# Softmax sums as identity matmuls in the logit bank, and a first inverse step of 64-partition matmuls in two banks

## The chip, the core and the metric

The kernel runs on one core of one Trainium2 chip. The engines that matter are TensorE (matmuls, PE in the profile; its weight loads are PEld), VectorE (DVE), ScalarE (ACT), GpSimd (POOL) and SyncE (SP), whose queue issues nearly all DMA transfers. Matmul results land in PSUM, a memory of eight banks of 2 KB for each of 128 partitions; VectorE and ScalarE read them from there. The metric is device time in microseconds of one execution, and the median of several runs is quoted.

## What is computed

Four layers on x of 2048 positions by 512 channels: attention, convolution, attention, convolution, each added to its layer-normed input. Cut to what the change touches:

```python
# attention: 32 heads of 16, each position looks at itself and at 7 earlier ones, 2 apart
qkv = (x @ wqkv).reshape(B, S, 3, H, Dh)
idx = pos[:, None] - off[None, :]              # off = 0, 2, ..., 14
logits = einsum("bhsd,bhswd->bhsw", q, kg) * scale
attn = softmax(where(mask, logits, -1e9), axis=-1)   # over the 8 keys w
o = einsum("bhsw,bhswd->bhsd", attn, vg)
return o @ wo
# convolution: y = irfft(rfft(u, 2L) * rfft(K, 2L))[:L] + u * Dskip, per channel, L = 2048,
# K = Re sum_n C_n exp(dt A_n l) dt B_n
```

Both attention layers share their weights, and both convolutions share the kernel K.

## The kernel before

**Start (0 to 112 us).** `k_gen` builds the taps K with powers of exp(dt A) and, in between, the first layer's norm, keys and queries. The order of all engines but GpSimd is written out by hand, one letter for each step (ORDERK here; ORDER0, ORDERF, ORDER1 for the convolutions).

**Attention (`LayerA.core`).** A block q is 512 positions, held as four rows of 128 partitions (a position's row is its index modulo 16, so rows 2 apart hold neighbours in the window). The program order is the order on each engine. For blocks 0 to 2, in slots (q, ft) with ft = 0 to 3: `mult` (L295, VectorE) multiplies queries with 8 shifted keys into `prod`; `lsum` (L302, TensorE) sums each head's 16 channels into the logits `L`, a PSUM tile of two banks laid out (row, key w, head), two tiles in turn; projections of values and queries (L351, L185) are put between. One block behind, `mx` takes the maximum over the keys (L365, VectorE), `sub_exp` subtracts it by an identity matmul (L372) and exponentiates into `ex` (L375, ScalarE), `recip` sums `ex` over the keys and makes rs = exp(-ln(sum)) (L381, L383, L385 on VectorE, L386 and L388 on ScalarE), and `norm_p` multiplies `ex` by rs into `attn` (L394, VectorE). For block q-1 `recip` stands after `lsum(q, 2)` and `norm_p` after `lsum(q, 3)`.

Then a loop over n = 0 to 15 goes through the rows, even ones mostly apart from odd ones at the start (0, 2, 1, 3, 4, ...): `pv_mult` (L404, VectorE, 2.28 us) multiplies weights and shifted values into `pav`, two buffers; `pv_sum` (L414, TensorE, 64 matmuls of 64 partitions, over two banks in turn) sums over the keys and transposes; ScalarE copies that to `oT` (L417); `out_proj` (L424, L426) projects it and adds x; ScalarE writes x back with its sums (L432, L108). Blocks 2 and 3 finish inside this loop: `recip` at n = 2 and n = 10, `norm_p` at n = 4 and n = 11. A position p x 16 + a lies in partition p of row a, so windows that reach back over row 0 need values of the partition before: two pairs of DMA copies `v_ext<-v_ext` (L356, L357), for even rows and for odd rows, each issued on SP when the last value projection of its kind is copied. The third pass of the loop (row 1) is the first that needs the odd ones. In layer 0 the loop also carries the loading and reordering of the taps (L1281, L1355) and sines for a table (L702).

**Convolution (`FftB`).** A transform of length 4096 in two steps each way. Channels come in two groups g of 256. K and U: `f1` (L758) copied by L747; k and u: `f2` (L765), copied by L747 or L820; m: `u_mult` (L807, VectorE) makes the products t1, t2 (the transform of the signal times that of the taps and its rotated partner, from the buffers `kf_ring`); y: `i1` (L833, L834), the first inverse step, 8 steps t to a group, copied to `z` by L747; z: `i2` (L857 to L859), the second inverse step, added to x (L862 on VectorE, or L864 on ScalarE with x added by an identity matmul). The letter after a token names the engine that copies: A ScalarE, D VectorE. "z01" is `i2` of group 0, quarter 1. All of these share accumulators of two banks each, four in turn, so step n waits until what step n-4 left has been copied out.

In a step of `i1` each of eight sets of four channels multiplies all 128 partitions of t1 and t2 with a table of 128 columns. Of these columns, each partition fills only the 32 that belong to its own channel of four (the mask `dmask_m`, L619, L666).

At the end of layer 0's convolution (ORDERF) the next attention layer's norm, transposes and key projections follow at once; layer 1's (ORDER1) ends with the stores of the output.

Of the kernel before, what the change touches and what calls it, by code (L numbers as in the profile page):

```python
# [10 lines left out]
ACT = mybir.ActivationFunctionType  # L11
ALU = mybir.AluOpType
# [3 lines left out]
BF16 = mybir.dt.bfloat16  # L16
# [4 lines left out]
P = 128  # L21
S = 2048
D = 512
H = 32
DH = 16
W = 8
# [15 lines left out]
DQT = 8  # L42
# [120 lines left out]
class LayerA:  # L163
# [143 lines left out]
    def core(self, x_sb, u, lnp, ev=None, nprod=0):  # L307

        tc, nc, lnst, l = self.tc, self.nc, self.lnst, self.layer
        ident, nident = self.c["ident"], self.c["nident"]  # L310
# [5 lines left out]
        st, linit, mult, lsum = self.st, self.linit, self.mult, self.lsum  # L316
# [5 lines left out]
        with ExitStack() as c2:  # L322
# [7 lines left out]
            wk = c2.enter_context(tc.tile_pool(name=f"a{l}_wk", bufs=2, reuse_waits="tile"))  # L330
# [45 lines left out]
                st[q]["ex"] = ex  # L376

            def recip(q):
                ex = st[q]["ex"]
                s4 = wk.tile([P, 4, 4, H], BF16, name="s4", bufs=1)  # L380
                nc.vector.tensor_tensor(s4[:], ex[:, :, 0:4, :], ex[:, :, 4:8, :], ALU.add)  # L381
                s2 = wk.tile([P, 4, 2, H], BF16, name="s2", bufs=1)
                nc.vector.tensor_tensor(s2[:], s4[:, :, 0:2, :], s4[:, :, 2:4, :], ALU.add)  # L383
                ssum = wk.tile([P, 4, 1, H], F32, name="ssum")
                nc.vector.tensor_tensor(ssum[:], s2[:, :, 0:1, :], s2[:, :, 1:2, :], ALU.add)  # L385
                nc.scalar.activation(ssum[:], ssum[:], ACT.Ln)  # L386
                rs = wk.tile([P, 4, 1, H], BF16, name="rs", bufs=1)
                nc.scalar.activation(rs[:], ssum[:], ACT.Exp, scale=-1.0)  # L388
                st[q]["rs"] = rs
# [114 lines left out]
            rows = [0, 2, 1, *range(3, NA)]  # L504
            for n in range(16):
# [3 lines left out]
                if n in (2, 10):  # L509
                    recip(2 + n // 8)  # L510
# [72 lines left out]
def iota_f32(nc, pool, name, n, step=1, base=0, channel_multiplier=0, parts=P):  # L583
    ti = pool.tile([parts, n], I32, name=name + "_i")
    nc.gpsimd.iota(ti[:], pattern=[[step, n]], base=base, channel_multiplier=channel_multiplier)
    tf = pool.tile([parts, n], F32, name=name)
    nc.scalar.copy(tf[:], ti[:])
    return tf


def build_b_consts(nc, cpool, tmp, w2_dram):
    C = {}
    EQ = P // 4
    base = tmp.tile([P, EQ, 16], I32, name="w2_base", tag="w2_base")
    pi_i = tmp.tile([P, 1], I32, name="p_i")
    nc.gpsimd.iota(pi_i[:], pattern=[[0, 1]], base=0, channel_multiplier=1)
    e21 = iota_f32(nc, tmp, "e21", P, step=256, base=128)
    aidx = iota_f32(nc, tmp, "aidx", 16, step=4096)
    d4i = iota_f32(nc, tmp, "d4i", 4)
    nc.gpsimd.iota(base[:], pattern=[[16, EQ], [4096, 16]], base=8, channel_multiplier=0)  # L600
    zt = tmp.tile([P, 1024], BF16, name="w2_zero")
    nc.gpsimd.memset(zt[:], 0.0)
    t_i = tmp.tile([P, 8], I32, name="pk_t")
# [2 lines left out]
    nc.vector.tensor_scalar(t_i[:, 2:3], pi_i[:], 3, None, ALU.bitwise_and)  # L606
    nc.vector.tensor_scalar(t_i[:, 3:4], pi_i[:], 31, 1, ALU.bitwise_and, ALU.logical_shift_right)
    nc.vector.tensor_scalar(t_i[:, 4:5], pi_i[:], 1, None, ALU.bitwise_and)
    nc.vector.tensor_scalar(t_i[:, 5:6], pi_i[:], 5, None, ALU.logical_shift_right)
    nc.vector.tensor_scalar(t_i[:, 6:7], pi_i[:], 63, 1, ALU.bitwise_and, ALU.logical_shift_left)  # L610
    nc.vector.tensor_copy(t_i[:, 7:8], pi_i[:])
    pk = tmp.tile([P, 8], F32, name="pk"); nc.vector.tensor_copy(pk[:], t_i[:])
# [2 lines left out]
    aux = cpool.tile([P, 8], F32, name="aux")  # L615
    nc.vector.tensor_tensor(aux[:, 0:1], pk[:, 6:7], rik, ALU.add)
    nc.vector.tensor_scalar(aux[:, 1:2], pf, 2.0, 1.0, ALU.mult, ALU.add)
    C["p21"] = aux[:, 1:2]
    dmask_m = aux[:, 4:8]  # L619
    nc.vector.tensor_scalar(dmask_m, d4i[:], d4m, 2.0 / 4096.0, ALU.is_equal, ALU.mult)  # L620

    f1t = [tmp.tile([P, P], I32, name=f"f1_t{j}") for j in range(2)]
# [8 lines left out]
    def rest():  # L631
# [14 lines left out]
        ws, w2q = {}, {}  # L646
# [15 lines left out]
            sine(ws[name][:], low16(wt[name][:].rearrange("p r a -> p (r a)")))  # L662

        def w_mask(name):
            C[name] = cpool.tile([P, 32, 4], BF16, name=name)
            nc.gpsimd.tensor_tensor(C[name][:], ws[name][:].unsqueeze(2).to_broadcast([P, 32, 4]),  # L666
                                    dmask_m.unsqueeze(1).to_broadcast([P, 32, 4]), ALU.mult)

        def w2_store():
            for s in range(4):  # L670
# [5 lines left out]
        steps += [lambda nm=nm, t=t: f1_sine(nm, t) for nm, t in zip(("F1c", "F1s"), f1t)]  # L676
        steps += [w2_sine] + [lambda name=name: w_sine(name) for name, offs in wps]
        C["masks"] = lambda: [w_mask(name) for name, offs in wps]
        return steps, w2_store

# [27 lines left out]
class FftB:  # L708
# [113 lines left out]
    def i1(self, g, t, eng):  # L822
        nc, C = self.nc, self.C
        if t == 0:
            self.S[g]["z"] = self.z0 if g == 0 else self.gtile("z", [P, 2 * NA, DQG * 4])
        z = self.S[g]["z"]
        t1, t2 = self.S[g]["t"]
        wp_r = C["Wp"][:].rearrange("p m d -> p (m d)")
        wpj_r = C["WpJ"][:].rearrange("p m d -> p (m d)")
        p3 = self.ptile([P, DQT, P])  # L830
        for j in range(DQT):
            dql = t * DQT + j
            nc.tensor.matmul(p3[:, j, :], lhsT=t1[:, dql, :], rhs=wp_r, start=True, stop=False)  # L833
            nc.tensor.matmul(p3[:, j, :], lhsT=t2[:, dql, :], rhs=wpj_r, start=False, stop=True)  # L834
        self.evac(z[:, :, t * DQT * 4:(t + 1) * DQT * 4].rearrange("p m (j d) -> p m j d", d=4),
                  p3[:].rearrange("p j (m d) -> p m j d", d=4), eng)

    def i2(self, g, t, eng):

# [447 lines left out]
def kernel(  # L1287
# [38 lines left out]
    with tc.manual_schedule(engines=MAN):  # L1326
        C = k_gen(tc, nc, consts["ident"], ins, kd, la, x_v, lnst, lambda sp: build_b_consts(nc, cpool, sp, w2_dram))
# [153 lines left out]
```

## Time and profile before

| what | us |
|---|---|
| median of 3 runs (424.58 to 425.59) | 424.74 |
| the profiled execution, whole | 425.23 |
| its span, first to last instruction | 423.40 |
| VectorE busy | 396.5 |
| TensorE matmuls busy | 337.9 |
| ScalarE busy | 321.7 |
| L381, L383, L385 (VectorE, 8 each), median of one | 0.418, 0.293, 0.292 |
| L833, L834 (TensorE, 256 each), mean of one | 0.219 |
| L747 into z on ScalarE (12), on VectorE (4), mean of one | 1.03, 1.22 |

Matmuls are pipelined: one takes 0.219 us from start to end, but the next starts well before. What a row of them costs is read from start to start. A line of the timeline gives start, length, engine, line, operation, output and input, and in brackets how long the engine had been idle and what ended that. The stretches that matter: 118 to 141 the logits of layer 0, 141 to 197 its loop, 199 to 262 the first convolution, 262 to 316 front and logits of layer 1, 314 to 372 its loop, 373 to 419 the second convolution.

### The profile page before, as it was taken

How to read it: one execution, taken by the hardware profiler on the slowest of the kernel's cores; microseconds unless marked ns; L12 is line 12 of the kernel's file. 1: busy time of each engine (PE TensorE's matmuls, PEld its weight loads, DVE VectorE, ACT ScalarE, POOL GpSimd, SP SyncE). 2: the span in 40 equal slices, each digit the busy share in tenths (PEclk: the TensorE clock that was granted, in tenths of full speed). 3: DMA queues.
4: the chain of work that ended last, by engine and by line, in shares of the span. 5: the costliest groups of instructions: out<-in, count | busy, mean ns of one | idle time of the engine just before them, and what ended most of it. 6: DMA issues, size and time to landing. Idle time of an engine off the chain costs nothing.

```text
span 423.4 us, 14780 instructions
## 1 busy us (share of the span) xinstructions
PE 337.9 (80%) x6530; PEld 239.4 (57%) x6530; DVE 396.5 (94%) x539; ACT 321.7 (76%) x552; POOL 43.9 (10%) x46
## 2 busy tenths in 40 slices
PE   3000179999999879779998999999997878996995
PEld 2000036657765555546887898555654655576894
DVE  8999999999999999997999958889899999989975
ACT  5999998986455478987999988764555658679962
POOL 3000300000499000000500000000000020000000
PEclk9999999999999898999999999999999999999999
DMA  8940742122014855393244692730033036515406
GB/s 205 394 121 12 76 85 70 32 59 70 18 43 116 219 149 169 103 378 104 78 152 178 224 324 58 241 108 2 2 98 79 3 145 269 185 59 165 137 17 185
DMA packets 62458, 54.30 MB, mean 128 GB/s; under 512 B 33877, under 2 KB 50874, under 8 KB 61114
## 3 DMA queue, kind: packets, MB, share of 16 engines
q1 hardware_dynamic: 62250, 53.22, 41.4%
q8 instruction: 51, 0.84, 0.9%
q10 hardware_dynamic: 144, 0.13, 0.3%
q14 instruction: 13, 0.11, 0.1%
HBM read 30.28 MB, written 13.24 MB: 103 GB/s over the span
## 4 chain that ended last, share of the span: by engine, by line
PE 33%; DVE 28%; ACT 8%; DMA 6%; SPq 5%; issue 5%; DVEq 0%; ACTq 0%
DVE pav L404 11%; DVE t L807 5%; PE pk L1176 4%; DVE a1s L747 4%; PE pp L1114 4%; PE pq L351 3%; PE pp L242 3%; SPq L1198 3%; PE L L302 2%; PE pq L185 2%; PE pb L834 2%; PE pb L833 2%; PE pq L426 2%; PE po L414 2%; DMA kf_ring<-kf_dram 2%
## 5 line engine op out<-in xcount | busy, mean ns | idle before, releaser
L404 DVE TENSOR_TENSOR pav<-attn,v_ext 128x4096 bf16<-128x4096 bf16 x32 | 72.9, 2282 | 0.2 <-PE pq L426 0.2
L295 DVE TENSOR_TENSOR prod<-qT,kT_ext 128x4096 bf16<-128x4096 bf16 x29 | 66.4, 2307 | 0.2
L414 PE MATMUL po<-ident,pav 64*128 64x64 bf16 x2048 | 36.6, 192 | 16.8 <-DVE pav L404 10.9
L414 PEld LDWEIGHTS <-pav 64*128 64x128 bf16 x2048 | 33.2, 96 | 28.8 <-DVE pav L404 22.0
L1104 PE MATMUL pt<-ident,x_blk 128*128 128x128 bf16 x64 | 6.8, 259 | 43.1 <-ACT x_blk L158 43.1
L1016 DVE TENSOR_TENSOR A_t<-A_t,pow_t 128x1024 bf16<-128x1024 bf16 (+4 forms) x46 | 38.3, 874 | 0.2
L426 PE MATMUL pq<-wop,oT 128*128 128x512 bf16 x128 | 34.6, 395 | 0.0
L820 ACT CAST ub<-pb 128x1024 bf16<-128x1024 f32 x32 | 32.5, 1056 | 1.4 <-DVE t L807 0.6
L353 ACT CAST v_ext<-pq 128x512 bf16<-128x512 f32 x32 | 18.7, 586 | 19.3 <-PE pq L351 18.1
L302 PEld LDWEIGHTS <-prod 128*128 128x128 bf16 x928 | 26.7, 96 | 9.5 <-DVE prod L295 4.8
L1114 PE MATMUL pp<-xnT,kT_ext 128*128 128x512 bf16 x96 | 29.2, 436 | 3.4 <-ACT xnT L1107 1.7
L1104 PEld LDWEIGHTS <-x_blk 128*128 128x128 bf16 x64 | 5.5, 118 | 46.0 <-ACT x_blk L158 44.0
L765 PE MATMUL pb<-a1s,w_sb 128*128 128x64 bf16 x768 | 27.3, 193 | 5.2 <-ACT a1s L747 2.9
L833 PE MATMUL pb<-Wp,t 128*128 128x128 bf16 x256 | 30.4, 219 | 1.2 <-ACT xnT L747 0.5
L834 PE MATMUL pb<-WpJ,t 128*128 128x128 bf16 x256 | 30.0, 219 | 1.1 <-DVE t L807 1.1
L351 PE MATMUL pq<-wv,xnT 128*128 128x512 bf16 x128 | 30.7, 379 | 0.0
L747 DVE CAST a1s<-pb 128x1024 bf16<-128x1024 f32 x23 | 27.0, 1213 | 3.8 <-PE pb L758 3.8
L765 PEld LDWEIGHTS <-w_sb 128*128 128x128 bf16 x768 | 24.7, 98 | 7.5 <-issue 5.8
L302 PE MATMUL L<-ind,prod 128*128 128x8 bf16 x928 | 27.5, 166 | 1.3 <-DVE prod L295 1.1
L747 ACT CAST a1s<-pb 128x1024 bf16<-128x1024 f32 x25 | 24.9, 1036 | 2.5 <-PE pb L758 2.2
L834 PEld LDWEIGHTS <-t 128*128 128x128 bf16 x256 | 24.9, 98 | 3.2 <-DVE t L807 1.5
L417 ACT CAST oT<-po 128x512 bf16<-128x512 f32 x32 | 18.4, 576 | 9.7 <-PE po L414 9.4
(227 smaller groups left out, 864.4 us busy)
## 6 DMA issues: line engine op xcount, KB each, us to landing
w_sb<-w_dram SPq DMA_DIRECT2D x8, 1024.0 KB, 7.3
w_dram<-w_zero SPq DMA_DIRECT2D x1, 4096.0 KB, 14.4
kf_ring<-kf_dram SPq DMA_DIRECT2D x13, 256.0 KB, 3.7
kf_ring<-kf_dram SPq DMA_DIRECT2D x26, 128.0 KB, 3.6
v_ext<-v_ext SPq DMA_DIRECT2D x4, 784.0 KB, 6.3
x_blk<-in_A_x_dram SPq DMA_DIRECT2D x4, 512.0 KB, 4.3
kT_ext<-in_A_wqkv_dram SPq DMA_DIRECT2D x4, 512.0 KB, 9.3
x_sb<-in_A_x_dram SPq DMA_DIRECT2D x4, 512.0 KB, 7.0
```

The costliest lines, as they stand in the source:

```text
L295: nc.vector.tensor_tensor(pr, self.qT[q][:, ft].unsqueeze(1).to_broadcast([P, W, 4, P]), kap, ALU.mult)
L302: self.nc.tensor.matmul(L[:, al, w, ft * 8:(ft + 1) * 8], lhsT=pr[:, w, al, :], rhs=self.c["ind8"][:], start=(ft == 0 and w == 0 and al % ...
L351: nc.tensor.matmul(pp[:], lhsT=xnT[:, dt, a * P:(a + 1) * P], rhs=wv[:, dt, :], start=(dt == 0), stop=(dt == NDT - 1))
L404: nc.vector.tensor_tensor(pv[:], attn[:, n % 4].unsqueeze(2).to_broadcast([P, W, DH, H]), vap, ALU.mult)
L414: nc.tensor.matmul(po[:, h, 0, ft, :], lhsT=pvf[rows, w, ft * P:(ft + 1) * P], rhs=ident[rows, rows], start=(w == 0 and ft == 0), stop=(w ...
L426: nc.tensor.matmul(pw[:], lhsT=oT[:, ftp, :], rhs=self.wo[:, ftp, :], start=False, stop=(ftp == NDT - 1))
L747: (self.nc.scalar.copy if eng == "act" else self.nc.vector.tensor_copy)(dst, src)
L765: nc.tensor.matmul(p2[:, j, :], lhsT=self.w2[:, ec * EC + j, :], rhs=a1s[:, ec * EC + j, :], start=True, stop=True)
L833: nc.tensor.matmul(p3[:, j, :], lhsT=t1[:, dql, :], rhs=wp_r, start=True, stop=False)
L834: nc.tensor.matmul(p3[:, j, :], lhsT=t2[:, dql, :], rhs=wpj_r, start=False, stop=True)
L1016: return lambda: nc.vector.tensor_tensor(*args)
L1114: nc.tensor.matmul(pps[kind, b, ft][:], lhsT=la.wqk[:, dt, c:c + P], rhs=la.xnT[:, dt, b * 512:(b + 1) * 512], start=(dt == 0), stop=(dt = ...
```

## The change

The three VectorE adds in `recip` go. In their place eight matmuls with the identity add the eight keys of `ex` in PSUM, into the first 128 columns of the block's own logit tile, whose content `ex` has replaced. The Ln on ScalarE reads the sum from there.

In `i1` each matmul of 128 partitions and 128 columns becomes two, of partitions 0 to 63 and 64 to 127 and of 64 columns, with the outputs in two different banks. The table has 64 columns: of a half's partitions each fills the 32 of its own channel of two. The mask and the copies to `z` follow the new layout.

With the smaller tiles the buffers behind them take other addresses, and with them the waits of some DMA issues: in SP's queue of layer 1 the load of `g2_sb` now stands ahead of the `kf_ring` loads, and two of those loads stand between the two pairs of `v_ext` copies. The order on the compute engines is as before but for the instructions named.

```diff
--- before.py
+++ after.py
@@ -376,14 +376,12 @@
                 st[q]["ex"] = ex
 
             def recip(q):
-                ex = st[q]["ex"]
-                s4 = wk.tile([P, 4, 4, H], BF16, name="s4", bufs=1)
-                nc.vector.tensor_tensor(s4[:], ex[:, :, 0:4, :], ex[:, :, 4:8, :], ALU.add)
-                s2 = wk.tile([P, 4, 2, H], BF16, name="s2", bufs=1)
-                nc.vector.tensor_tensor(s2[:], s4[:, :, 0:2, :], s4[:, :, 2:4, :], ALU.add)
+                ex, L = st[q]["ex"], st[q]["L"]
+                tot = L[:, 0, 0:4, :]
+                for w in range(W):
+                    nc.tensor.matmul(tot, lhsT=ident[:], rhs=ex[:, :, w, :], start=(w == 0), stop=(w == W - 1), skip_group_check=True)
                 ssum = wk.tile([P, 4, 1, H], F32, name="ssum")
-                nc.vector.tensor_tensor(ssum[:], s2[:, :, 0:1, :], s2[:, :, 1:2, :], ALU.add)
-                nc.scalar.activation(ssum[:], ssum[:], ACT.Ln)
+                nc.scalar.activation(ssum[:, :, 0, :], tot, ACT.Ln)
                 rs = wk.tile([P, 4, 1, H], BF16, name="rs", bufs=1)
                 nc.scalar.activation(rs[:], ssum[:], ACT.Exp, scale=-1.0)
                 st[q]["rs"] = rs
@@ -596,7 +594,7 @@
     nc.gpsimd.iota(pi_i[:], pattern=[[0, 1]], base=0, channel_multiplier=1)
     e21 = iota_f32(nc, tmp, "e21", P, step=256, base=128)
     aidx = iota_f32(nc, tmp, "aidx", 16, step=4096)
-    d4i = iota_f32(nc, tmp, "d4i", 4)
+    d4i = iota_f32(nc, tmp, "d4i", 2)
     nc.gpsimd.iota(base[:], pattern=[[16, EQ], [4096, 16]], base=8, channel_multiplier=0)
     zt = tmp.tile([P, 1024], BF16, name="w2_zero")
     nc.gpsimd.memset(zt[:], 0.0)
@@ -606,7 +604,7 @@
     nc.vector.tensor_scalar(t_i[:, 2:3], pi_i[:], 3, None, ALU.bitwise_and)
     nc.vector.tensor_scalar(t_i[:, 3:4], pi_i[:], 31, 1, ALU.bitwise_and, ALU.logical_shift_right)
     nc.vector.tensor_scalar(t_i[:, 4:5], pi_i[:], 1, None, ALU.bitwise_and)
-    nc.vector.tensor_scalar(t_i[:, 5:6], pi_i[:], 5, None, ALU.logical_shift_right)
+    nc.vector.tensor_scalar(t_i[:, 5:6], pi_i[:], 5, 1, ALU.logical_shift_right, ALU.bitwise_and)
     nc.vector.tensor_scalar(t_i[:, 6:7], pi_i[:], 63, 1, ALU.bitwise_and, ALU.logical_shift_left)
     nc.vector.tensor_copy(t_i[:, 7:8], pi_i[:])
     pk = tmp.tile([P, 8], F32, name="pk"); nc.vector.tensor_copy(pk[:], t_i[:])
@@ -616,7 +614,7 @@
     nc.vector.tensor_tensor(aux[:, 0:1], pk[:, 6:7], rik, ALU.add)
     nc.vector.tensor_scalar(aux[:, 1:2], pf, 2.0, 1.0, ALU.mult, ALU.add)
     C["p21"] = aux[:, 1:2]
-    dmask_m = aux[:, 4:8]
+    dmask_m = aux[:, 4:6]
     nc.vector.tensor_scalar(dmask_m, d4i[:], d4m, 2.0 / 4096.0, ALU.is_equal, ALU.mult)
 
     f1t = [tmp.tile([P, P], I32, name=f"f1_t{j}") for j in range(2)]
@@ -662,9 +660,9 @@
             sine(ws[name][:], low16(wt[name][:].rearrange("p r a -> p (r a)")))
 
         def w_mask(name):
-            C[name] = cpool.tile([P, 32, 4], BF16, name=name)
-            nc.gpsimd.tensor_tensor(C[name][:], ws[name][:].unsqueeze(2).to_broadcast([P, 32, 4]),
-                                    dmask_m.unsqueeze(1).to_broadcast([P, 32, 4]), ALU.mult)
+            C[name] = cpool.tile([P, 32, 2], BF16, name=name)
+            nc.gpsimd.tensor_tensor(C[name][:], ws[name][:].unsqueeze(2).to_broadcast([P, 32, 2]),
+                                    dmask_m.unsqueeze(1).to_broadcast([P, 32, 2]), ALU.mult)
 
         def w2_store():
             for s in range(4):
@@ -825,15 +823,16 @@
             self.S[g]["z"] = self.z0 if g == 0 else self.gtile("z", [P, 2 * NA, DQG * 4])
         z = self.S[g]["z"]
         t1, t2 = self.S[g]["t"]
-        wp_r = C["Wp"][:].rearrange("p m d -> p (m d)")
-        wpj_r = C["WpJ"][:].rearrange("p m d -> p (m d)")
-        p3 = self.ptile([P, DQT, P])
+        p3 = self.ptile([P, 2, DQT, 64])
         for j in range(DQT):
             dql = t * DQT + j
-            nc.tensor.matmul(p3[:, j, :], lhsT=t1[:, dql, :], rhs=wp_r, start=True, stop=False)
-            nc.tensor.matmul(p3[:, j, :], lhsT=t2[:, dql, :], rhs=wpj_r, start=False, stop=True)
-        self.evac(z[:, :, t * DQT * 4:(t + 1) * DQT * 4].rearrange("p m (j d) -> p m j d", d=4),
-                  p3[:].rearrange("p j (m d) -> p m j d", d=4), eng)
+            for tt, w, first in ((t1, C["Wp"], True), (t2, C["WpJ"], False)):
+                for h in range(2):
+                    rows = slice(64 * h, 64 * h + 64)
+                    nc.tensor.matmul(p3[:, h, j, :], lhsT=tt[rows, dql, :], rhs=w[rows].rearrange("p m d -> p (m d)"),
+                                     start=first, stop=not first)
+        self.evac(z[:, :, t * DQT * 4:(t + 1) * DQT * 4].rearrange("p m (j h d) -> p m j h d", h=2, d=2),
+                  p3[:].rearrange("p h j (m d) -> p m j h d", d=2), eng)
 
     def i2(self, g, t, eng):
```

## The prediction

> **What bounds the kernel now.** I read busy time by engine, then by stage, then the chain that ended last, then each engine's timeline in the stages that the change touches. First the engines, and six stages (columns: stretch, length, busy time and count on PE, PEld, DVE, ACT, POOL, then TensorE clock, DMA share, GB/s).
>
> ```profile
> PE 337.9 (80%) x6530; PEld 239.4 (57%) x6530; DVE 396.5 (94%) x539; ACT 321.7 (76%) x552; POOL 43.9 (10%) x46
> ...
> 140.00:200.00 60.00, 50.34 (x1347) 32.38 (x1349) 56.83 (x54) 46.85 (x98) 1.02 (x1) 0.94 0.60 190
> 234.00:245.15 11.15, 10.20 (x207) 9.58 (x202) 11.09 (x18) 11.12 (x14) 0.00 (x0) 1.00 0.61 225
> 245.15:254.60 9.45, 9.45 (x149) 9.21 (x150) 4.89 (x7) 7.60 (x9) 0.35 (x1) 1.00 1.04 342
> 284.00:316.00 32.00, 31.95 (x477) 19.40 (x474) 29.71 (x23) 17.09 (x31) 0.00 (x0) 1.00 0.11 30
> 322.60:372.00 49.40, 41.27 (x1116) 25.91 (x1114) 48.92 (x55) 33.44 (x86) 2.89 (x1) 0.97 0.39 141
> 403.40:417.30 13.90, 13.87 (x189) 13.16 (x190) 10.36 (x10) 6.90 (x8) 0.00 (x0) 1.00 0.24 72
> ```
>
> VectorE is the busiest on average, but the limit changes by stage: the two attention loops (140 to 200, 322.6 to 372) are VectorE's, with ScalarE close behind in the first; 284 to 316 is TensorE's; the ends of the convolutions (245 to 255, 403 to 417), where the inverse steps stand, are TensorE's too. So each half of the change must be priced stage by stage, not by its busy time.
>
> **Part 1: sums over the keys.** Removed, eight times (four blocks in two layers): three VectorE adds.
>
> ```profile
> 324.84 0.42 DVE L381 TENSOR_TENSOR s<-ex 128x512 bf16<-128x512 bf16 x1
> 325.29 0.29 DVE L383 TENSOR_TENSOR s<-s 128x256 bf16<-128x256 bf16 x1
> 325.62 0.29 DVE L385 TENSOR_TENSOR ssum<-s 128x128 f32<-128x128 bf16 x1
> 325.83 2.29 DVE L404 TENSOR_TENSOR pav<-attn,v_ext 128x4096 bf16<-128x4096 bf16 x1
> ```
>
> From the first add to the next product is 0.99 us of VectorE; eight of them about 9.6 us busy (4.2 + 3.1 + 8 x 0.292 for L381, L383 and L385). Added: 64 TensorE matmuls of 128 columns. L833 and L834, also 128 columns with a weight load each, start 0.056 us apart:
>
> ```profile
> 245.60 0.06 PE pb L833
> 245.66 0.06 PE pb L834
> ```
>
> so one block costs 8 x 0.056 = 0.45 us of TensorE. The Ln then reads the bank instead of SBUF. No row has that form; the nearest are 0.31 us (L386, 128 elements from SBUF) and 0.58 us (L417, 512 elements from a bank). I take 0.31, the nearer in size; eight times the difference, of which at most two lie on the path, would be 0.5 us.
>
> Layer 0. Blocks 0 and 1 fall at 123.6 and 136.3, where VectorE and TensorE are both full. VectorE gets ahead, but the path into the loop is TensorE's value projections and then a transfer: the second v_ext copy is issued at 140.15 and 140.83 and its second half takes 7.8 us to land (the DMA view's row for 105 KB), that is 148.63; the third pav starts at 148.72.
>
> ```profile
> 140.83 0.90 SPq L357 DMA_DIRECT2D v_ext<-v_ext  x1
> 148.72 2.29 DVE L404 TENSOR_TENSOR pav<-attn,v_ext 128x4096 bf16<-128x4096 bf16 x1
> 159.17 1.11 PE L414 MATMUL po<-ident,pav 64*128 64x64 bf16 x64 [1.76 <-ACT oT L417]
> ```
>
> Before that projection TensorE gets 2 x 0.45 = 0.90 more work, and wins back about 0.54 of waits on prod (0.34 at 127.72, 0.20 at 134.27): the copy is 0.4 us later. Block 2 (1.0 us of VectorE at 150.93) is then hidden, because from 153 to 173.8 the chain runs through ScalarE (table load, sines, oT; TensorE waits 1.76 for oT at 159.17) and reaches VectorE again at the maximum at 173.83. Block 3 (180.11) is on the path, but the copies to oT after 187 on ScalarE are back to back and hold TensorE at 192.77, so I count 0.4 of its 1.0. Sum for layer 0: -0.4 + 0.4 = 0.0. Ends: -1.0 if no wait is won back and block 3 is hidden; +2.0 if the transfer does not hold the loop.
>
> Layer 1. In 284 to 316 TensorE is idle for 0.05 us, so blocks 0 and 1 cost 0.90 us, and the second v_ext copy, the attention weights of block 1 and the loop start that much later. In the loop VectorE has no wait: block 2 gives 1.0. Block 3's Ln starts at 355.03 though its sum ended at 353.71, since ScalarE is full from 351.16 to 358.4. So the weights of block 3 can come at about 355.7 instead of 356.15: 0.45 gained. Sum: -0.90 + 1.0 + 0.45 = 0.55; ends -0.9 and +1.1.
>
> The Ln is now behind TensorE, which behind it has the projections and pv_sum. The exponentials that it waits for were finished 2 us or more earlier in all eight places (319.92 for block 2, needed near 323.4), so nothing queues there. The bank stays taken until the Ln, but its next writer comes at least 2 us later (303.46 in layer 1, block 2).
>
> **Part 2: the inverse step.** Removed: 512 matmuls of 128 rows by 128 columns, 16 to a step at 0.0555, 0.89 us a step. Added: 1024 of 64 rows by 64 columns. The kernel already runs that form, alternating over two banks, in pv_sum:
>
> ```profile
> 334.71 1.03 PE L185 MATMUL pq<-xnT,kT_ext 128*128 128x512 bf16 x4
> 335.67 1.11 PE L414 MATMUL po<-ident,pav 64*128 64x64 bf16 x64
> 336.70 0.39 PE L424 MATMUL pq<-x_sb,ident 128*128 128x512 bf16 x1
> ```
>
> 64 of them take 1.03 us from start to start, 0.0161 each: 32 make 0.52 us, 0.37 less a step, 11.8 us over 32 steps. The four L185 stream 4 x 0.216 = 0.86, so pv_sum starts 0.10 us late on entering the 64-row form; the two entries on each path cost 0.2. "TensorEngine Tiling (Array Packing)", Key Properties, in the Trainium skill speaks against the change here: a switch of tiling mode drains the array. It gives no figure; an estimate by it, with one whole 0.22 us matmul (L833) exposed at each of the four entries, would take a further 0.5 us from the gain.
>
> What the path keeps is less, since the copies out of the banks stay as long. Most steps run while ScalarE (234 to 245) or VectorE (372 to 403) sets the pace, and there the gain is nothing. At the ends it counts.
>
> ```profile
> 243.20 3.89 ACT L747 CAST xnT<-pb 128x1024 bf16<-128x1024 f32 x4
> 246.81 4.01 ACT L747 CAST z<-pb 128x1024 bf16<-128x1024 f32 x4
> 252.43 1.93 ACT L747 CAST z<-pb 128x1024 bf16<-128x1024 f32 x2 [1.60 <-PE pb L834]
> ```
>
> Layer 0: the last product ends at 245.09, then TensorE does eight steps and z01, and z00 ends at 254.6. ScalarE copies every 0.91 us from 243.20; with TensorE ahead it no longer waits 1.60 at 252.43, so the last two copies start at 250.45 and 251.36; the last step needs the accumulator freed at 250.56, and ends at 251.2; z00 (12 x 0.11 = 1.31) ends at 252.5. That is 2.1 less, less one entry's part: 1.9. What follows (statistics, transposes, keys) is a TensorE chain without gaps up to 316, so it is kept. The weights for it landed by 257.5, when DMA goes quiet, and are needed at 263.8: cover enough.
>
> Layer 1: VectorE's own copies (403.30 to 405.64, then at 405.57, 407.55, 408.7, 409.8) hold the accumulators. z00 needs z01's freed at 409.9, against a start of 412.28 now: again 1.9 with an entry. Ends for each: 1.0 and 2.6 (all of 8 x 0.37, less entries).
>
> **Off the path.** The masks Wp and WpJ are half as wide on GpSimd (2.9 us now, done long before 234). One 1 MB load (g2_sb) moves in SP's queue from 367.84 to just ahead of the kf_ring loads (263.8 to 277), and two kf_ring loads fall between the two v_ext copies (306 and 316). Cover: the ring is first read at 381.77; the first v_ext copy lands about 6.5 us after 306.2, needed at 314.6. Without that cover it would cost up to 1.2 us (two issues of 0.6).
>
> **Sum.** 0.0 + 0.55 + 1.9 + 1.9 = 4.35 us. The profiled execution took 425.23 us, 423.40 of it span; the median is 424.74, 0.49 below. Taken from the median: 424.74 - 4.35 = 420.4. With all low ends 424.74 - (-1.0 - 0.9 + 2.0) = 424.6, with all high ends 424.74 - (2.0 + 1.1 + 5.2) = 416.4; they won't fall together.
>
> **The rivals.**
> 1. VectorE's time is gained whole: blocks 2 and 3 of both layers give 4.0, and the lead into layer 0's loop 1.35 (attention weights of block 1 at 138.95 for 140.31). For it: VectorE is busy 94%. Against it: the transfer at 148.63 and ScalarE's chain. 424.74 - (3.8 + 5.35 - 0.9) = 416.5.
> 2. The halves don't run side by side: 32 x 0.027 (64 columns at half the spacing of 128) = 0.87 a step, as now. For it: the two halves of a step add to the same place two matmuls later, in pv_sum eight later. Against it: L833 and L834 add back to back at 0.056. Part 1 alone: 424.74 - 0.55 = 424.2.
> 3. Slower: the copy out now takes pairs from two banks in turn. Place: L747 and the z copies, eleven on ScalarE before z00 in layer 0, some four before 245 and five in layer 1, 20 on the path. Price: 20 e for e more a copy; it decides from e = 4.35 / 20 = 0.22, a copy of 1.24 us. At e = 0.3 the time is 424.74 - 4.35 + 6.0 = 426.4. For it: some ScalarE copies take 1.14 (kf_nat). Against it: copies with one element at a time (a1s) take 1.04 and 1.21, as z does.
>
> **How the numbers follow.** Forecast 0.62, rival 1 0.14, rival 2 0.13, rival 3 0.11. About 0.3% (1.3 us) is what a measurement can tell from no change. Faster: 0.61 + 0.14 + 0.03 = 0.78; same: 0.01 + 0.10 + 0.02 = 0.13; slower 0.09. Range 416.6 to 424.0: most of rival 1 and the near half of rival 2 inside, the rest and rival 3 out, some 0.19. The forecast's own range is 418.5 to 422.5.
>
> **What would show it.** Right: L381 to L385 gone and eight 128-column matmuls per block 0.056 apart; the inverse matmuls 0.016 apart; ScalarE without a wait of 1.6 before the last z copies of layer 0; z00 of layer 1 some 4.4 us earlier than 412.28 and the third pav of layer 0 not earlier than 148.7. Wrong: copies longer than 1.1 us, matmul pairs at 0.05, or a new wait of VectorE for rs beyond 0.6 us.

## The result, and the profile after

| kernel | median us (runs) | ratio to before, 95% interval |
|---|---|---|
| changed, first comparison | 418.94 (4) | 0.9857 [0.984, 0.9874] |
| changed, again, beside three experiments | 420.60 (6) | 0.9905 [0.9868, 0.9941] |

Before took 425.09 (4 runs) in the first and 424.63 (17 runs) in the second, so the change takes off 6.2 or 4.0 us; the forecast, 4.35 off, lies between. The two intervals overlap only from 0.9868 to 0.9874; why the first comparison came out lower stays open. The profiled execution of the changed kernel took 418.89, its span 417.1 against 423.4. In two experiments below some executions were disturbed (half of e_halves', the profiled one among them, and two of e_pad's twelve); their ratios leave these out, their medians do not.

Busy time by engine and by stage in the changed kernel (columns as in the prediction's first fence):

```profile
PE 320.5 (77%) x7048; PEld 231.5 (55%) x7106; DVE 387.9 (93%) x515; ACT 321.7 (77%) x552; POOL 37.7 (9%) x46
...
243.26:251.16 7.90, 7.12 (x276) 6.18 (x277) 4.41 (x6) 7.68 (x9) 0.35 (x1) 1.00 1.01 327
281.00:312.50 31.50, 31.08 (x435) 19.01 (x441) 26.39 (x17) 16.29 (x29) 0.00 (x0) 1.00 0.15 39
320.00:367.00 47.00, 38.34 (x1117) 26.18 (x1130) 46.64 (x48) 32.83 (x83) 2.89 (x1) 1.00 0.35 126
```

TensorE lost 17.4 us and VectorE 8.6. From the end of the first convolution's last product to ScalarE's first copy to x_sb is 7.90 here, 9.54 before (245.09 to 254.63). ScalarE carries that stretch now: 7.68 of 7.90 busy.

ScalarE's timeline at the end of the first convolution:

```profile
245.18 5.76 ACT L745 CAST z<-pb 128x1024 bf16<-128x1024 f32 x6
251.16 1.01 ACT L863 CAST x_sb<-pb 128x1024 bf16<-128x1024 f32 x1 [0.21 <-PE pb L858]
```

Six copies back to back, 0.96 each: the wait of 1.60 is gone, and a copy that takes pairs from two banks is no longer than before (on ScalarE a median of 1.02 in both kernels). TensorE's timeline as it enters an inverse step:

```profile
247.66 0.27 PE L858 MATMUL pb<-xnT,g_sb 128*128 128x256 bf16 x1
247.87 0.20 PE L832 MATMUL pb<-Wp,t 64*128 64x64 bf16 x2
247.91 0.19 PE L832 MATMUL pb<-WpJ,t 64*128 64x64 bf16 x2
247.94 0.19 PE L832 MATMUL pb<-Wp,t 64*128 64x64 bf16 x2
```

"x2" is a pair, one matmul for each half, and pairs are 0.03 apart: 0.015 to 0.016 a matmul. The 256-column one takes 0.11 from start to start, so 0.21 to the first pair is an entry 0.10 late, as forecast. "TensorEngine Tiling (Array Packing)", Key Properties, in the Trainium skill says that a change of tiling mode drains TensorE and gives no figure; whatever drain there is here lies within this 0.10.

VectorE's timeline, first before at the start of layer 0's logits, then in the changed kernel, both layers' logits and the start of layer 0's loop:

```profile
113.10 4.80 DVE L295 TENSOR_TENSOR prod<-qT,kT_ext 128x4096 bf16<-128x4096 bf16 x2
118.07 1.23 DVE L365 TENSOR_REDUCE mx<-L 128x128 bf16<-128x1024 f32 x1 [0.17 <-PE L L285]
```

```profile
114.87 4.49 DVE L295 TENSOR_TENSOR prod<-qT,kT_ext 128x4096 bf16<-128x4096 bf16 x2 [2.07 <-PE L L302]
119.28 1.22 DVE L365 TENSOR_REDUCE mx<-L 128x128 bf16<-128x1024 f32 x1
...
139.30 0.69 DVE L392 TENSOR_TENSOR attn<-ex,rs 128x1024 bf16<-128x1024 bf16 x1 [0.72 <-ACT rs L386]
139.91 2.29 DVE L402 TENSOR_TENSOR pav<-attn,v_ext 128x4096 bf16<-128x4096 bf16 x1
...
147.84 4.49 DVE L402 TENSOR_TENSOR pav<-attn,v_ext 128x4096 bf16<-128x4096 bf16 x2
...
298.55 0.69 DVE L392 TENSOR_TENSOR attn<-ex,rs 128x1024 bf16<-128x1024 bf16 x1 [1.29 <-ACT rs L386]
...
311.69 0.69 DVE L392 TENSOR_TENSOR attn<-ex,rs 128x1024 bf16<-128x1024 bf16 x1 [1.29 <-ACT rs L386]
```

Three things to see. At 114.87, ahead of any changed instruction, VectorE waits 2.07 for TensorE; before it did not, and its first maximum is 1.2 late (119.28 for 118.07). The third pav comes at 147.84: the forecast said not before 148.7. And VectorE waits for rs more than the 0.6 that the forecast allowed: 0.72 in layer 0, where before it did not wait, and 1.29 twice in layer 1, for 0.54 before.

Where the 6.3 us of span come from, as marks in the two traces (before, after, gain). "Weights" are the products `attn`; `a1s` is what the first matmuls of a convolution are copied to, so its first copy marks the end of the loop:

| mark | before | after | gain so far |
|---|---|---|---|
| first pav, layer 0 | 140.91 | 139.91 | 1.0 |
| weights of block 3, layer 0 | 183.62 | 180.55 | 3.1 |
| first a1s copy, convolution 0 | 199.00 | 196.73 | 2.3 |
| first product of layer 1 | 279.61 | 276.15 | 3.5 |
| first pav, layer 1 | 314.59 | 312.30 | 2.3 |
| first a1s copy, convolution 1 | 373.84 | 369.46 | 4.4 |
| first copy from z00, convolution 1 | 413.36 | 407.00 | 6.4 |

So one profile gives layer 0's sums 2.3, its inverse steps and the rest of the convolution 1.2, layer 1's sums 0.9, its inverse steps 2.0. The experiments ask which of these stand.

### The profile page after: what moved, and what is told of

Its sections match the earlier page's. It is cut to its first block, busy times and chain, and to the rows that moved or that the text cites. A ratio compares the mean times of both kernels' runs of the same rounds, so it can differ in the third digit from the quotient of the medians.

```text
span 417.1 us, 15864 instructions
## 1 busy us (share of the span) xinstructions
PE 320.5 (77%) x7048; PEld 231.5 (55%) x7106; DVE 387.9 (93%) x515; ACT 321.7 (77%) x552; POOL 37.7 (9%) x46
## 4 chain that ended last, share of the span: by engine, by line
PE 35%; DVE 21%; ACT 14%; issue 5%; DMA 5%; SPq 3%; DVEq 0%; ACTq 0%
PE pq L351 6%; DVE pav L402 5%; DVE t L805 5%; PE L L302 4%; DVE a1s L745 4%; PE pk L1175 4%; PE pq L185 3%; DVE prod L295 3%; PE pp L242 3%; PE po L412 3%; PE pp L1113 3%; PE pq L424 2%; SPq L1280 2%; DMA w_sb<-w_dram 2%; ACT ub L818 1%
## 5 line engine op out<-in xcount | busy, mean ns | idle before, releaser
L412 PE MATMUL po<-ident,pav 64*128 64x64 bf16 x2048 | 36.3, 190 | 15.1 <-DVE pav L402 7.7
L1103 PE MATMUL pt<-ident,x_blk 128*128 128x128 bf16 x64 | 7.0, 260 | 43.4 <-ACT x_blk L158 43.4
L424 PE MATMUL pq<-wop,oT 128*128 128x512 bf16 x121 | 31.7, 379 | 4.3 <-issue 3.8
L763 PE MATMUL pb<-a1s,w_sb 128*128 128x64 bf16 x768 | 28.4, 196 | 6.2 <-ACT a1s L745 2.9
L763 PEld LDWEIGHTS <-w_sb 128*128 128x128 bf16 x768 | 25.8, 100 | 8.6 <-issue 6.8
L1113 PE MATMUL pp<-xnT,kT_ext 128*128 128x512 bf16 x87 | 25.0, 406 | 6.2 <-ACT qT L1118 3.3
L1175 PEld LDWEIGHTS <-A_t 128*64 128x64 bf16 (+1 forms) x512 | 22.3, 105 | 3.6
L1175 PE MATMUL pk<-B_t,A_t 128*64 128x84 bf16 (+1 forms) x512 | 24.1, 203 | 0.1
L832 PE MATMUL pb<-Wp,t 64*128 64x64 bf16 x512 | 19.4, 192 | 5.9 <-ACT ub L818 2.8
```

The lines of the kernel that those rows point to most:

```text
L412: nc.tensor.matmul(po[:, h, 0, ft, :], lhsT=pvf[rows, w, ft * P:(ft + 1) * P], rhs=ident[rows, rows], start=(w == 0 and ft == 0), stop=(w ...
L424: nc.tensor.matmul(pw[:], lhsT=oT[:, ftp, :], rhs=self.wo[:, ftp, :], start=False, stop=(ftp == NDT - 1))
L763: nc.tensor.matmul(p2[:, j, :], lhsT=self.w2[:, ec * EC + j, :], rhs=a1s[:, ec * EC + j, :], start=True, stop=True)
L1113: nc.tensor.matmul(pps[kind, b, ft][:], lhsT=la.wqk[:, dt, c:c + P], rhs=la.xnT[:, dt, b * 512:(b + 1) * 512], start=(dt == 0), stop=(dt = ...
L1175: nc.tensor.matmul(o, lhsT=lhs, rhs=Bt[:, ri, c * CH + ql].rearrange("p b g -> p (b g)"), start=(not half and j % 4 == 0 and ri == 0), sto ...
```

## The experiments

All are timed against the kernel before; e_after, e_best, e_no_l0 and e_xearly share one comparison (before 424.63), as do the first four (424.82) and the last four (424.81).

| kernel | median us (runs) | ratio, 95% interval |
|---|---|---|
| e_soft | 423.85 (12) | 0.9975 [0.9959, 0.9991] |
| e_inv | 422.55 (12) | 0.9948 [0.9926, 0.9971] |
| e_gap | 420.09 (6) | 0.9867 [0.9835, 0.99] |
| e_lead1 | 418.80 (4) | 0.9849 [0.9826, 0.9873] |
| e_after | 420.60 (6) | 0.9905 [0.9868, 0.9941] |
| e_best | 418.14 (6) | 0.9837 [0.9805, 0.987] |
| e_no_l0 | 421.89 (12) | 0.9931 [0.9909, 0.9952] |
| e_xearly | 420.70 (6) | 0.9890 [0.9856, 0.9923] |
| e_pad | 424.05 (12) | 0.9958 [0.9937, 0.9979] |
| e_bestpad | 421.54 (6) | 0.9919 [0.9904, 0.9935] |
| e_halves | 428.42 (12) | 0.9997 [0.9964, 1.003] |
| e_l0lead | 421.32 (12) | 0.9933 [0.991, 0.9957] |

### The two parts alone

e_soft is before with the new `recip`, e_inv the changed kernel with the old one:

```diff
 # e_inv
-                for w in range(W):
-                    nc.tensor.matmul(tot, lhsT=ident[:], rhs=ex[:, :, w, :], start=(w == 0), stop=(w == W - 1), skip_group_check=True)
...
+                nc.vector.tensor_tensor(s4[:], ex[:, :, 0:4, :], ex[:, :, 4:8, :], ALU.add)
...
```

> The softmax part alone, on the kernel before. What the forecast put on record for it is 0.55 us less than before (about 424.4). Read from the two traces, layer 0 brings 1.8 (the last product of its convolution ends 245.09 before, 243.26 after) and layer 1 0.9 (first a1s copy of the second convolution 4.4 earlier, its first product 3.46 earlier), so 2.7 less: about 422.3, and the third pav of layer 0 near 147.8. If VectorE's time were gained whole (the forecast's rival 1) it is 4.45 less: about 420.5.

> The inverse step alone, on the kernel before. Forecast 3.8 less than before. Read from the two traces 1.64 in layer 0 and 1.98 in layer 1, 3.6 less: about 421.4, if the two parts of the change add up. If the inverse steps gain only because the softmax part let the copies ahead of them run earlier, it is well under that, 2.5 or less: above 422.4.

Measured: 1.0 off and 2.3 off. Neither met its expectation read from the two traces, and the inverse step missed the forecast too (3.8). At 422.55 e_inv falls on the side of its rival (above 422.4), that the inverse steps gain less without the sums. Its trace shows other reasons: TensorE idle for 0.87 at 251.36 with nothing named, and a half clock from 403 to 407 in the second convolution. Together the parts make 3.2, against 4.0 or 6.2 for both: within the interval of the second comparison they add up, and the first profile flattered the change. VectorE's time gained whole (4.45 for the sums) is out.

### The changed kernel again

> The changed kernel once more, on the chip that runs the three others of this comparison. In the six profiles so far TensorE's granted clock falls to 0.50 for about 3.5 us at a time, in one to four places a run, and not in the same places (before: 143, 160, 347; changed kernel: 65, 386, 416; the changed kernel with room added: also 157, 243, 345, 400). If these spells alone make the scatter, the time is again 418.5 to 420 and the profile shows other places; a spell in the copies before z00 of layer 0 (243 to 247) costs about 0.8, as the second copy to x_sb there is 2.55 and 3.24 earlier with one and 3.47 without.

Measured 420.60, 0.6 above the range expected. The falls of the clock are easy to see by single microseconds; here from the changed kernel with room added, in the inverse steps of convolution 0 (third number from the end: granted clock):

```profile
242.00:243.00 1.00, 0.39 (x14) 0.28 (x16) 0.76 (x2) 1.00 (x3) 0.00 (x0) 1.00 0.40 152
243.00:244.00 1.00, 1.00 (x50) 1.00 (x44) 0.00 (x0) 1.00 (x3) 0.00 (x0) 0.50 1.00 383
244.00:245.00 1.00, 1.00 (x46) 1.00 (x42) 0.43 (x1) 1.00 (x2) 0.34 (x1) 0.50 1.02 377
```

In e_after they lie at 65, 157, 345 and 417, in the first profile of the same program at 65, 386 and 416. The two together differ by 1.4 at the first product of layer 1, 277.56 and 276.15, with the same instructions. Marks of one profile are therefore worth about a microsecond, and each term below is taken from several.

The places are not free. In each of the fourteen profiles all falls after 60 us begin on one grid of 3.413 us (in e_after at 65.60, 157.76, 345.50 and 417.18: 27, 55 and 21 steps apart), and in the step ahead of each, 62 in all, TensorE's matmuls and weight loads fill at most 0.70 of the time; not every such step is followed by a fall. The offset of the grid from the first instruction differs between executions, so the same program meets its falls elsewhere.

### Layer 0's sums

e_no_l0 puts VectorE's adds back in all of layer 0, e_l0lead in its blocks 0 and 1:

```diff
+            def recip(q):
+                (recip_v if l == 0 else recip_t)(q)              # e_no_l0
+                (recip_v if l == 0 and q < 2 else recip_t)(q)    # e_l0lead
```

`recip_v` holds VectorE's adds, `recip_t` the matmuls.

> The changed kernel with VectorE's adds in all four blocks of layer 0, identity matmuls in layer 1 alone. The difference to the changed kernel is what the softmax part brings in layer 0. The forecast put 0.0 on it (time 418.9); the traces say 1.2 to 2.3, most likely 1.8 (about 420.7); with VectorE's time gained whole it would be 3.35 (422.3).

> The changed kernel with VectorE's adds in blocks 0 and 1 of layer 0, ahead of its loop; blocks 2 and 3 and layer 1 stay on TensorE. Theory: the layer's gain (1.3 in the comparison without any identity matmuls in it) comes half from ahead of the loop and half in it: the first pav at 140.8 for 140.0, the third at 148.5 or later, the maximum of block 3 to the weights of block 3 in 8.8 as in the changed kernel: 0.4 to 0.9 more than the changed kernel. Rival (the forecast): the second v_ext copy holds the loop, so nothing is lost and the third pav stays where it is, 147.8.

Measured: e_no_l0 1.3 above the changed kernel in the same comparison, the low end of 1.2 to 2.3, and not the forecast's 0.0. Their two intervals overlap, so the times alone don't prove it; the marks, three profiles against seven, do. At the first a1s copy, profiles with adds in layer 0 stand at 198.55 to 199.00 (three), those with matmuls in all four blocks and neither a load nor transposes moved or added at 196.03 to 197.82 (e_best, e_gap, the changed kernel twice, e_lead1, e_halves, e_soft). e_l0lead is between at 197.90, as in time (421.32, from another comparison); its third pav comes at 147.99, not at 148.5 or later, but everything from its first product on is 0.5 earlier than in e_no_l0, and from there to that pav both take 35.54.

The step that gave 0.0 was the transfer: 140.83 + 7.8 = 148.63 holds the loop. The landing of the second v_ext copy before, and in e_no_l0, which has the same adds; ahead of it in each the issue of the x_sb load on SP's queue:

```profile
137.59 1.59 SPq L1360 DMA_DIRECT2D x_sb<-in_A_x_dram  x1
...
DMA to landing us min/median/max: 7.8/7.8/7.8
```

```profile
134.51 0.60 SPq L1375 DMA_DIRECT2D x_sb<-in_A_x_dram  x1
140.67 0.90 SPq L357 DMA_DIRECT2D v_ext<-v_ext  x1
...
DMA to landing us min/median/max: 6.1/6.1/6.1
```

With the same code the load was issued 3.1 earlier, and the copy took 6.1 and landed at 146.8, well ahead of the pav. e_inv has 6.2, e_l0lead 5.7. The 7.8 belonged to one execution. What holds the third pav is VectorE's own row of work, in e_no_l0:

```profile
144.08 2.28 DVE L418 TENSOR_TENSOR pav<-attn,v_ext 128x4096 bf16<-128x4096 bf16 x1
146.28 2.28 DVE L295 TENSOR_TENSOR prod<-qT,kT_ext 128x4096 bf16<-128x4096 bf16 x1
148.48 2.28 DVE L418 TENSOR_TENSOR pav<-attn,v_ext 128x4096 bf16<-128x4096 bf16 x1
```

No idle time stands ahead of any of them. Only when the sums leave VectorE does the copy begin to hold it, by 0.19 in the changed kernel and 0.50 in e_lead1.

Of the loop's part, block 2's 1.0 hangs on the clock. From the weights of block 2 to the maximum of block 3 is 15.1 in e_no_l0 and 16.0 in e_after, where it is given back: TensorE runs at 0.50 from 157.8 to 161.2, ScalarE waits for it, and so does the maximum in the end. ScalarE's and VectorE's timelines in e_after:

```profile
161.97 0.60 ACT L430 ACTIVATE x_sb<-pq 128x512 bf16<-128x512 f32 x1 [0.85 <-PE pq L424]
...
172.79 1.22 DVE L365 TENSOR_REDUCE mx<-L 128x128 bf16<-128x1024 f32 x1 [0.83 <-PE L L285]
```

In the changed kernel's first profile, the only one with matmuls there and no fall of the clock between 157 and 164, neither wait stands, it is 15.1 and the 1.0 is kept; in the ten others it is 16.0 to 17.1. With adds such a fall costs little: before has one from 160.2 to 163.6 and 15.3. Block 3 is kept whole: from that maximum to the weights is 9.78 in e_no_l0 and 8.80 in e_after, and from the weights to the first a1s copy 15.38 in both.

### A buffer that moved, and the lead of layer 1

```diff
 # e_gap, layer 0's work pool
-                wk.tile([P, 1024], BF16, name="gap", bufs=1)
+                wk.tile([P, 1024 + 768], BF16, name="gap", bufs=1)
 # e_lead1
+                (recip_v if l == 1 and q < 2 else recip_t)(q)
 # e_best: both
```

> The changed kernel with 1536 bytes of unused room ahead of the work tiles of layer 0, so that the buffers behind them lie where they lay in the kernel before. Theory: the first prod waited 2.07 us for TensorE at 114.87 since its buffer now lies on one that TensorE was still reading (A_pr); the wait goes, the first maximum comes about 1.2 earlier (118.1 for 119.28), and the weights of block 1 up to 1.2 earlier. What reaches the end is held by the landing of the second v_ext copy (third pav at 147.84 after a wait of 0.19): 0 to 0.5 less than the changed kernel, 418.4 to 418.9. Rival: the wait is one for TensorE's order of work and not for memory: nothing moves.

> The changed kernel, with blocks 0 and 1 of layer 1 summed by VectorE's adds again (blocks 2 and 3, and layer 0, stay on TensorE). Theory: 284 to 316 is TensorE's, so the 16 matmuls there cost what the first pav of layer 1 lost (3.46 earlier at the first product, 2.29 at the pav: 1.17); without them 1.0 to 1.2 less than the changed kernel, 417.8. Rival: VectorE is as full there as TensorE with the copies of the maximum and the products, and its six adds take the time back: 418.9 or more.

> Both side experiments together: room of 1536 bytes in layer 0's work pool, and VectorE's adds again for blocks 0 and 1 of layer 1. Theory: the first maximum of layer 0 1.2 earlier and the third pav some 0.5 earlier, and 1.2 off the lead of layer 1 (first product to the first pav of layer 1 35.0 long, as before, for 36.15): 417.3, 1.0 to 1.7 less than the changed kernel in this comparison. Rival: what the lead gains is lost in the loops behind it, as ScalarE and the transfers set their pace: within 0.5 of the changed kernel.

VectorE's timeline in e_gap, to be held against 114.87 and 119.28 above:

```profile
113.09 4.80 DVE L295 TENSOR_TENSOR prod<-qT,kT_ext 128x4096 bf16<-128x4096 bf16 x2
118.06 1.23 DVE L365 TENSOR_REDUCE mx<-L 128x128 bf16<-128x1024 f32 x1 [0.16 <-PE L L285]
```

The wait of 2.07 is gone, with no instruction changed but the place of a buffer: s4 and s2, which the change deleted, held 1536 bytes, and without them the product's buffer lay on one that TensorE still read. The first pav comes at 139.36 for 139.91. The time, 420.09, misses the 418.4 to 418.9 expected and does not show it (the clock falls at seven places in that profile).

In e_lead1, from the first product of layer 1 to its first pav is 34.98, in the changed kernel 36.15, before 34.98: the 16 matmuls in TensorE's full stage cost 1.17, as expected; from that product to the first a1s copy of the second convolution is 92.29, 93.31 and 94.23. The time, 418.80, is 6.0 off; 417.8 was expected, and 418.9 or more if VectorE's adds took the gain back. Beside the changed kernel's two medians it decides nothing, so the marks carry this.

Both together, 418.14, are 2.5 below the changed kernel on the same chip (expected 1.0 to 1.7); the two intervals, [0.9805, 0.987] and [0.9868, 0.9941], only just touch. It is the lowest median of the study, and its profile has the shortest span:

```profile
span 416.1 us, 15835 instructions
```

### The x_sb load

```diff
-        ev = {("v", 0): [lambda: x_load((0,))], ("v", 1): [lambda: x_load((1, 2, 3))], ...
+        ev = {("m", 1, 0): [lambda: x_load((0,))], ("v", 1): [lambda: x_load((1, 2, 3))], ...
```

> The kernel with both side experiments, and the first 512 KB load of x_sb issued ahead of the first v_ext copy of layer 0 in place of behind it. Theory: the second v_ext copy lands late because that load is ahead of it: 7.8 us before, where the load ended its issue 1.0 us ahead of the copy, 6.2 after, where it was 4.8 us; with the load gone the third pav of layer 0 has no wait for the copy (0.19 and 0.50 in the runs so far) and the time is 0.2 to 0.5 less than without the move. Rival: the three loads behind the copy hold it, and nothing changes.

It missed. SP issues the load at 130.31, right ahead of the first v_ext copy and not well ahead of it, and now that copy is late; VectorE's timeline (the name is of the transfer that came last):

```profile
140.66 2.29 DVE L418 TENSOR_TENSOR pav<-attn,v_ext 128x4096 bf16<-128x4096 bf16 x1 [1.72 <-DMA wop<-in_A_wo_dram]
```

The first pav waits 1.72, to 140.66 for 138.93 in e_best, and the time is 2.6 above e_best. That a copy behind this load lands late holds: the second copy of this pair takes 8.8 us to land, where the first takes 5.8 to 6.3 in the other thirteen profiles. The move only shifted which copy it is.

### TensorE without instructions

In several profiles TensorE stops in the middle of 64-row matmuls for nothing that the trace names. Here in e_after, TensorE's timeline in convolution 0, and then queue q8 in the DMA view of 247.3 to 247.4 (packets, MB, share of 16 engines' time):

```profile
248.77 0.19 PE L832 MATMUL pb<-WpJ,t 64*128 64x64 bf16 x2
249.78 0.20 PE L832 MATMUL pb<-Wp,t 64*128 64x64 bf16 x2 [0.81 <-issue]
249.80 0.21 PE L832 MATMUL pb<-WpJ,t 64*128 64x64 bf16 x2
```

```profile
q8 instruction: 1, 0.02, 58.2%
```

The stall of 0.81 ends 2.4 us after an instruction packet started. q8 over the whole run, before and then changed:

```profile
q8 instruction: 51, 0.84, 0.9%
```

```profile
q8 instruction: 55, 0.90, 0.9%
```

Four more packets for 576 more weight loads, each with its matmul (6530 to 7106 loads): q8 feeds TensorE, 128 to 129 such couples to a packet (e_pad, with 64 more, has 56 packets). To move the packets against the work:

```diff
+        spare = pst.tile([P, 4, P], BF16, name="pt")
+        for _ in range(64):
+            nc.tensor.transpose(spare[:, 0, :], raw["C_im"][:, 0, :], ident[:])
```

> The changed kernel with 64 extra transposes into an unread tile early on (TensorE is idle from 8 to 50 us), so 128 more TensorE instructions ahead of everything. In ten profiles TensorE stands still for 0.8 us or more in the middle of 64-row matmuls, with nothing shown that it waits for, and seven such stalls end 2.4 to 2.8 us after an instruction packet starts on queue q8 (251.46 after 248.7, 251.36 after 248.8, 249.78 after 247.3, 252.03 after 249.6; before: 191.12 after 188.5; changed kernel: 182.31 after 179.8 and 188.5 after 185.8). TensorE has 14,214 instructions and 55 packets, some 258 each, so the packets behind the extra ones come half a packet sooner. Theory (late instructions): the stalls leave their places, at 249 to 252 and 182 to 191, for others half a packet away, and again end 2.4 to 2.8 us after a packet. Rival (the place itself: its banks, its operands or the transfers of that stage): the stalls stay at the same instructions. The time is 419 to 422 either way.

> The kernel with both side experiments (room in layer 0's work pool, VectorE's adds for blocks 0 and 1 of layer 1) and the same 64 extra transposes. If late instructions are the cause, other stalls than in that kernel's profile (there 0.35 at 187.19 and none at 249 to 252) and a time up to 1 us either side of its 418.1; if place is the cause, the same profile and time.

In e_pad the stalls of 182 to 191 are gone, and that of convolution 0 comes 64 matmuls (half a packet) later in the work, ahead of the 509th of the 512 short ones there for the 445th, after a packet at 249.9:

```profile
252.19 0.20 PE L832 MATMUL pb<-Wp,t 64*128 64x64 bf16 x2 [1.24 <-issue]
```

In e_bestpad one of 1.18 at 251.46 stands where e_best had none, after a packet at 249.2; one of 0.23 is left at 191.86. The fourteen traces hold 38 such stalls of 0.2 or more inside a row of 64-row matmuls. All end 2.2 to 2.8 after a packet's start, and counted in weight loads from the start of the program all end 88 to 92 past a multiple of 128. So does the stall of convolution 0: ahead of the 445th short matmul in e_after, e_gap, e_lead1 and e_xearly, of the 461st in e_l0lead (16 matmuls fewer in front of it), of the 477th in e_inv and e_no_l0 (32 fewer). So they go with the packets and not with the place. The times missed: 424.05 is 3.4 above the changed kernel and 421.54 as much above e_best, where 419 to 422 and about 418 were expected. After the 64 transposes the clock stays at 0.50 from 19 to 67 us in e_pad (to 61 in e_bestpad), but its first maximum, at 119.06, is not late; the loss comes later, spread over the stages (1.0 by the first a1s copy, 2.2 at the end), and its cause stays open.

"Runtime: NRT & Kernel Launch", Instruction fetch mechanics, in the Trainium skill says that instructions come in blocks of 16 KiB, 256 each, and that the crossing is mostly hidden. Size and number agree (0.90 MB in 55 packets); here it is not hidden. A likely reason, not tested apart: 128 couples of weight load and matmul at 0.0161 use up a packet in 2.1 us, less than the 2.2 to 2.8 from a packet's start to the end of the stall, where 128-column ones at 0.0555 take 7.1. Why the stall at one count is 0.8 long in one execution and not there in another stays open.

### Halves in turn, or one after the other

```diff
-            for tt, w, first in ((t1, C["Wp"], True), (t2, C["WpJ"], False)):
-                for h in range(2):
+        for h in range(2):
+            for j in range(DQT):
+                for tt, w, first in ((t1, C["Wp"], True), (t2, C["WpJ"], False)):
...
```

> The changed kernel with the 32 matmuls of an inverse step in another order: 16 of one half of the partitions, then 16 of the other, in place of by turns. Theory: two 64-row matmuls run side by side only when neighbours use different halves; alone each takes half of the 0.056 of a 128-column one, 0.027 to 0.03, a step 0.9 as before the change (the price of the forecast's rival 2), and the 1.98 gained at the end of layer 1 is lost again, with some 1 in layer 0: 2 to 3 us more than the changed kernel, 422.6 to 423.6. Rival: 64 columns follow each other in 0.016 whatever their rows, and the time stays at 420.6.

TensorE's timeline in e_halves, in a stretch at full clock:

```profile
238.44 0.19 PE L832 MATMUL pb<-Wp,t 64*128 64x64 bf16 x1 [0.25 <-ACT xnT L745]
238.47 0.19 PE L832 MATMUL pb<-WpJ,t 64*128 64x64 bf16 x1
238.50 0.19 PE L832 MATMUL pb<-Wp,t 64*128 64x64 bf16 x1
```

Each now takes the 0.03 that a pair took, so the gain needs the turns: short matmuls alone bring none. Which part of the turns it is was not tested apart. With the order of the halves the order of the banks changes too, and the two adds to one place now follow each other directly. At the end of layer 1 (first a1s copy to the last add, at full clock) 43.3 becomes 44.6, of 45.3 before. The ratio, 0.9997, gives back all that the change brought; why this is more than the 2 to 3 us expected stays open.

## Why the prediction came out right

Either comparison lies inside the stated range, but that the sum comes so close to the second one is luck: two of its four terms were wrong by about as much in opposite directions.

- Layer 0's sums, 0.0: wrong; 1.3 by the times, 1.6 by the first a1s copy (198.55 in e_no_l0, 196.97 in e_after). e_soft's 1.0 for both layers together says that it may be less. The step that failed is "the second v_ext copy ... takes 7.8 us to land, that is 148.63; the third pav starts at 148.72". The two numbers stood beside each other by chance; VectorE had no idle time ahead of that pav, and the copy lands in 5.7 to 6.2 in the three other runs with adds in the lead. The lead into the loop was therefore gained, less the 2.07 wait from the moved buffer, which the forecast did not look for: from the first product to the third pav is 35.5 to 35.6 with adds in the lead and 34.1 to 34.2 in e_best and e_gap (34.7 in e_bestpad, where the copy does hold it, by 0.56). "Block 2 hidden" came out in ten of eleven profiles, but by the fall of the clock and not by ScalarE's chain alone; the trace that the forecast was read from has a fall in that place (160.2), and VectorE waits for nothing longer than 0.2 there from 158.5 to 173.8. Of block 3, 0.4 was counted and 1.0 came.
- Layer 1's sums, 0.55: right in size; 0.7 by the marks (from first product to first a1s copy 94.2 and 94.6 with adds; with matmuls 93.1 to 94.0 in seven profiles and 94.5 in e_pad, 93.7 on average), 0.7 by the times (e_inv to e_no_l0, across two comparisons). The lead cost 1.17 for 0.90. Block 3 (from its maximum to its weights, 9.44 before) gave 0.98 where the clock kept up (the changed kernel's first profile, e_no_l0, e_l0lead) and 0.44 to 0.69 in the nine profiles with a fall there. The 0.45 was read from a trace with one, at 347.9.
- Inverse steps of layer 0, 1.9: mis-sized. From the first product with kf_nat to the first product of layer 1, before has 41.82; eleven profiles with the new steps gain between -0.25 and 1.62, in the middle 0.64. The 1.6 is of the run without stall or fall of the clock there; the others lose to a stall (0.25 to 1.24), a clock of 0.50, or a late w_sb transfer (0.57 in e_after). The forecast had none of the three.
- Inverse steps of layer 1, 1.9: right. From the first a1s copy to the last add is 45.27 before and 43.28 to 43.30 in seven profiles, 2.0 less; 43.74 and 43.97 where the clock fell at 400 to 406, and 43.4 to 43.5 after the transposes. DMA is at 0.28 there (399 to 411), 1.01 in layer 0 (243 to 251).
- The price of the new form, 0.0161 a matmul and 0.10 an entry, and the unchanged copies: right. Rival 1 falls with e_soft (1.0 of 4.45), rival 2 with the pairs 0.03 apart, and e_halves shows its price; rival 3 with copies at 0.96.
- Of its own signs, z00 of layer 1 came 6.4 earlier for 4.4, and two failed: the third pav (147.84, earlier than 148.7) and the waits for rs (0.72 and 1.29, beyond 0.6). The first belongs to layer 0's term. The second stands in the leads: in layer 1, where TensorE is full, it goes with the 1.17; in layer 0 it did not stop the lead from gaining.

## What to carry to other kernels

A transfer that lands just ahead of an instruction does not hold it unless the engine stood idle until then: look for the bracket first, and at how that landing varies between runs. Before taking a wait in one trace as the kernel's own, look whether the clock fell there. Deleting tiles moves the buffers behind them, so look for new waits ahead of the first changed instruction. More and shorter matmuls also cost instructions; where they run back to back, ask how often the next packet of them comes.

## What had not been expected of the hardware

- TensorE stalls of up to 1.47 us (e_xearly, 191.60) that end 2.2 to 2.8 after an instruction packet starts and come only at one place in each 128 weight loads; one already stood in the kernel before (0.84 at 191.12, after 188.6).
- The granted clock falls to 0.50 for 3.41 us at a time (twice that in e_xearly, five times in e_halves), three to seven times after 60 us, the last as the program ends, on a grid of 3.413 us whose offset varies between executions. The three profiles without a fall between 157 and 164 are those with an offset of 0.14 to 0.42; the eleven others have 0.66 to 3.18. After 64 transposes at 8 us it stayed there for 41 and 48 us.
- The same two issues on SP's queue took 1.1 us in one execution and up to 2.6 in another (kn<-kf_sb, at 223.58 before and at 223.08 in e_soft).
